# Two mixers of a decode kernel: the Gelu tiles summed on VectorE, and the small work placed at half chunks

## The chip, the cores and the metric

The kernel runs on one core of one Trainium2 chip. The engines that matter here are TensorE (PE in the profile, with PEld for its weight loads), VectorE (DVE), ScalarE (ACT), GpSimd (POOL), and the 16 DMA engines, which bring data from the chip's memory into SBUF. All large loads are issued in program order on the queue of SyncE (SPq in the profile, q1 in its list of DMA queues). PSUM holds the banks that TensorE accumulates into. The metric is the device time of one execution in microseconds.

## The reference

Two layers, each an attention with a long K and V cache and a mixer, for one new token of two batch items:

```python
def _A_ref(x, k_cache, v_cache, wq, wo):
    q = (x @ wq).reshape(B, 1, 32, 128)                 # 32 heads, transposed to (B, heads, 1, 128)
    k = jnp.repeat(k_cache, 4, axis=1)                  # 8 K/V heads, 32768 keys of 128
    v = jnp.repeat(v_cache, 4, axis=1)
    p = _softmax(einsum("bhqd,bhkd->bhqk", q, k) * (128 ** -0.5))
    return einsum("bhqk,bhkd->bhqd", p, v).reshape(B, 1, 4096) @ wo
def _B_ref(x, w1, b1, w2, b2):                          # token mixing, one token, F = 1792
    h = _layernorm(x)                                   # (B, 1, 512)
    u = _gelu(einsum("bsd,sf->bdf", h, w1) + b1)        # (B, 512, 1792)
    return transpose(einsum("bdf,fs->bds", u, w2) + b2) # (B, 1, 512)
x = A_x
for layer in range(2):
    x = x + _A_ref(_layernorm(x), A_k_cache, A_v_cache, A_wq, A_wo)
    x = x + _B_ref(_layernorm(x), B_w1, B_b1, B_w2, B_b2)
```

Both layers use the same caches and weights, so each batch item and head is read twice, apart from what the kernel keeps on chip in between.

## The kernel before

**Units and chunks.** A unit is one layer, one batch item and one K/V head: 32 of them, in an order fixed by `units`. Each unit has 8 chunks of 4096 keys for K and 8 for V. A chunk is 2 MB. `k_chunk` (L416) multiplies the unit's four queries with a chunk, 16 products into one PSUM tile of scores for each of two groups of four chunks; after each group VectorE takes the maxima (L426). When all K of a unit is through, `max_1` and `max_2` find the maxima over all keys (L432, L436, L438, L442, L444), the scores are turned (L448) into the SBUF tiles S0 and S1, ScalarE exponentiates them (L453, or all at once L465 and L468), and `v_chunk` (L558) multiplies them with the V chunks, 16 products of 128x512 each into the PSUM bank `acc`. At the unit's end `out_1` sums four masked blocks of `acc` on VectorE (L526, L528, `add_blocks`), multiplies with a selector (L595) and divides (L597); `out_2` multiplies with the head's part of wo and accumulates four rows in the PSUM bank `rows` (`add_row`, L238). The query of a unit comes from `make_q`: products with wq (L340), a copy (L349), four transposing products (L352) and a copy.

**Memory.** SBUF has 13 cells of 2 MB in `mem` (and a rest). Most chunks are loaded two or four at a time (4 and 8 MB). Between the units N1 and N3 fewer cells are free, since weights and a part of the cache that both layers use stay on chip: there the loads are of one chunk, or of two half chunks where no whole cell has been free for long enough (`spread`, `half`). A load into a cell waits for the products that last read it, so the order of TensorE's work decides when the next loads can start.

**The changes of layer and batch.** N1 is the last unit of layer 0 of batch item 0, N2 that of layer 0 of batch item 1. After each the mixer has to run, and the next but one unit (N1 + 2, N2 + 2) needs its result for its query. The unit in between (N1 + 1, N2 + 1) can already be computed. In the stream of chunks its K comes behind the last V of N1 or N2, its V behind that, and the resident K chunk of the unit after (kept on chip from layer 0, so without a load) among them. Because `rows` carries both batch items, the mixer works on rows: `take_rows` copies `rows` to S1 (L609) and clears them (L610), `mix_1` puts the layer's input into the PSUM bank `bcast` on all partitions, `mix_2` adds the attention's result with a selector product (L641), takes the statistics of the layer norm (L644 to L649, the power on GpSimd, L630) and makes scale and bias columns. A Gelu tile (`hidden_tile`, L780) is one ScalarE operation on `bcast`, 128 hidden units by 512 channels, and there are 14 of them. `hidden_out` multiplies each with its column of w2 and accumulates in `rows` (L238 again). `mix_4` adds the result to `bcast` by a selector product (L792), copies it (L799) and takes the statistics (L801 to L804); `to_columns` (L304) turns it into the columns from which `make_q` works.

**The order of work.** There is no automatic scheduler: each engine runs its instructions in the order in which the program issues them. The last loop goes through the stream of chunks. For each it issues the load, then the chunk's products, advances the time `t` by one and issues whatever `at(time, f, ...)` has put there, by rank. The load of a chunk is issued when its turn in this stream comes; how far it runs ahead of the products is settled by when its cell is read out. In the mixers of N1 and N2 the numbers in `BURSTS` say how many of the 14 `hidden_out` products, each followed by a later Gelu, stand behind each K chunk. `ASIDE` shifts the V chunks of N1 + 1 and N2 + 1 to three places earlier in the stream, and `SOONER` brings two V loads of N2 ahead of two K loads.

Of the kernel before, what the change touches and what calls it, by code (L numbers as in the profile page):

```python
# [9 lines left out]
AF = mybir.ActivationFunctionType  # L10
# [18 lines left out]
ASIDE = 3  # L29
BURSTS = (0, 3, 3, 3, 4, 1)  # L30
# [14 lines left out]
def gqa_mixer_kernel(ctx: ExitStack, tc: tile.TileContext, x, kt, v, wqo, cols, out):  # L45
# [279 lines left out]
    def make_q(n, step, place=None):  # L325
# [40 lines left out]

    SOONER = {(N2, 6): (N2, 1), (N2 + 1, 0): (N2, 3)}
# [38 lines left out]
    def k_chunk(n, c):  # L406

        kc = k_at.pop((n, c))
        half, i = divmod(c, PACK)
        if i == 0:  # L410
            sc_ps[n, half] = pscore.tile([P, 512], F32, name="scores")
        for k in range(SUB):
# [10 lines left out]
        if i == PACK - 1:  # L423
# [123 lines left out]
    def v_chunk(n, c):  # L547
        very_last = n == NU - 1 and c == NCH - 1
        vc = v_at.pop((n, c))
# [5 lines left out]
        for q in range(quads):  # L555
# [8 lines left out]
            )  # L564
        if very_last:
            add_tiles()
# [220 lines left out]

    def mix_4(key):
# [8 lines left out]
        else:  # L797
            ysb[key] = row_tile()
            nc.vector.tensor_copy(ysb[key], p)  # L799
            st, mv, rs = ln_st[:, :6], ln_mv, ln_rs  # L800
            nc.vector.bn_stats(st, p)  # L801
            nc.vector.bn_aggr(mv, st)
            nc.vector.tensor_scalar_add(rs, mv[:, 1:2], EPS)
            nc.gpsimd.tensor_tensor(rs, rs, half_neg, op=ALU.pow)  # L804
            stats[key] = mv, rs
# [45 lines left out]
    for n in range(NU):  # L851
# [4 lines left out]
        if n:  # L856
            if n in (N1 + 2, N2 + 2):
                q0 = q1 = mixed[layer - 1, b]
                place = S[1]
            else:  # L860
                place = S[0] if n in (N2 + 1, N3 + 1) else None
                q0 = kbeg[n] - (10 if n == N3 + 1 else 6)
                q1 = q0 + 1
            q2 = q1 + 1
            assert q2 <= kbeg[n]
            at(q0, make_q, n, 0)
            at(q1, make_q, n, 1)
            at(q2, make_q, n, 2, place)
            if place is S[0]:
# [3 lines left out]
        if n in (N1 + 1, N2 + 1):  # L873
            at(kend, max_1, n, 0)
            at(kend, max_2, n)
            at(kend, exponentials_at_once, n, 0)
            t1 = mixed[units[n - 1][:2]] + 1
# [4 lines left out]
        else:  # L882
# [4 lines left out]
            if n == N2:  # L887
# [17 lines left out]
        at(vend if change else min(vend + 1, vbeg[n + 1]), out_1, n)  # L905
        at(vend if change or n == NU - 2 else vend + 2, out_2, n)
# [125 lines left out]
```

## Time and profile before

| | |
|---|---|
| runs | 2498.47, 2500.21, 2500.77 us; median 2500.21 |
| profiled execution | 2501.7 us, span 2499.9 us |
| TensorE, mean granted clock | 0.766 |
| TensorE busy | 1400.0 us, 56% of the span |
| VectorE busy | 222.9 us, 9% |
| ScalarE busy | 185.6 us, 7% |
| read from the chip's memory | 1063.81 MB |

Shares of time are of the profiled execution's span. In the page's section of 40 slices a slice is 62.5 us; the two mixers that the diff touches lie at about 1145 to 1195 us and 1337 to 1385 us. The rows of the profile that the argument uses are shown with the prediction. A row of the timeline has the start and the duration in us, the engine, the line, the operation, the tiles as output<-inputs, the shapes, the count, and in brackets the engine's idle time before it with what ended it. A row of a table by stretch has the stretch, its length, for PE, PEld, DVE, ACT and POOL the busy time with the number of instructions, the mean granted clock of TensorE, the busy share of the DMA engines, and the GB/s that they moved. A row of a group has its line, engine, operation, tiles and shapes, the count, the busy time with the mean of one in ns, and the engine's idle time before it with its releasers.

### The profile page before, as it was taken

How to read it: one execution, taken by the hardware profiler on the slowest of the kernel's cores; microseconds unless marked ns; L12 is line 12 of the kernel's file. 1: busy time of each engine (PE TensorE's matmuls, PEld its weight loads, DVE VectorE, ACT ScalarE, POOL GpSimd, SP SyncE). 2: the span in 40 equal slices, each digit the busy share in tenths (PEclk: the TensorE clock that was granted, in tenths of full speed). 3: DMA queues.
4: the chain of work that ended last, by engine and by line, in shares of the span. 5: the costliest groups of instructions: out<-in, count | busy, mean ns of one | idle time of the engine just before them, and what ended most of it. 6: DMA issues, size and time to landing. Idle time of an engine off the chain costs nothing.

```text
span 2499.9 us, 20566 instructions
## 1 busy us (share of the span) xinstructions
PE 1400.0 (56%) x9326; PEld 380.2 (15%) x9326; DVE 222.9 (9%) x610; ACT 185.6 (7%) x550; POOL 4.9 (0%) x17
## 2 busy tenths in 40 slices
PE   4545554645445554667667775465545554456547
PEld 1111111111111111111111111111111111111112
DVE  0000000000000000001111110000000000010102
ACT  0000000000000000001012010000000000011002
POOL 0000000000000000000000000000000000000000
PEclk8777777777777777879888887677778777777778
DMA  9999999999999999999999999999999999999996
GB/s 419 436 433 427 435 436 429 436 430 430 433 434 434 433 429 434 424 425 416 426 424 415 427 428 432 430 433 432 433 434 433 430 430 433 434 431 433 430 432 271
DMA packets 34656, 1065.14 MB, mean 426 GB/s; under 512 B 4101, under 2 KB 4105, under 8 KB 5002
## 3 DMA queue, kind: packets, MB, share of 16 engines
q1 hardware_dynamic: 34280, 1063.80, 99.1%
q8 instruction: 73, 1.20, 0.2%
q14 instruction: 13, 0.11, 0.0%
q10 hardware_dynamic: 290, 0.04, 0.0%
HBM read 1063.81 MB, written 0.00 MB: 426 GB/s over the span
## 4 chain that ended last, share of the span: by engine, by line
DMA 72%; PE 26%; DVE 1%; ACT 1%; issue 0%; SPq 0%; POOL 0%; ACTq 0%
DMA mem<-in_v_dram 37%; DMA mem<-in_kt_dram 35%; PE scores L416 11%; PE acc L558 11%; PE rows L238 1%; PE kept L340 1%; PE bcast L340 0%; ACT S L780 0%; PE small L595 0%; PE small L442 0%; PE small L587 0%; PE kept L737 0%; PE small L352 0%; PE bcast L641 0%; DVE S L528 0%
## 5 line engine op out<-in xcount | busy, mean ns | idle before, releaser
L416 PE MATMUL scores<-mem,small_sb 128*32 128x512 f32 x4096 | 636.8, 735 | 597.4 <-DMA mem<-in_kt_dram 596.9
L558 PE MATMUL acc<-mem,S 128*16 128x512 f32 x4088 | 615.5, 739 | 445.1 <-DMA mem<-in_v_dram 439.4
L416 PEld LDWEIGHTS scores<-mem,small_sb 128*32 128x32 f32 x4096 | 153.4, 129 | 983.9 <-issue 907.9
L453 ACT ACTIVATE S<-S,small_sb 128x128 f32<-128x128 f32 x240 | 123.6, 519 | 2096.9 <-DVE small_sb L444 1627.0
L558 PEld LDWEIGHTS acc<-mem,S 128*16 128x16 f32 x4088 | 134.8, 111 | 808.0 <-issue 678.8
L426 DVE TENSOR_REDUCE small_sb<-scores 128x1 f32<-128x512 f32 x64 | 44.2, 691 | 870.2 <-PE scores L416 870.2
L448 DVE STREAM_TRANSPOSE S<-scores 128x512 f32<-128x512 f32 x64 | 45.4, 710 | 129.4 <-PE acc L558 129.4
L238 PE MATMUL rows<-mem,small_sb 128*1 128x512 f32 (+1 forms) x276 | 50.5, 637 | 3.1 <-ACT mem L780 2.4
L340 PE MATMUL kept<-mem,small_sb 128*2 128x512 f32 x104 | 51.2, 618 | 1.7 <-DVE small_sb L266 1.7
L453 ACT ACTIVATION_READ_ACCUMULATOR S<-S,small_sb 128x1 f32 x240 | 44.8, 187 | 0.0
L438 DVE TENSOR_REDUCE small_sb<-small 1x4 f32<-1x128 f32 x32 | 8.8, 276 | 271.7 <-PE small L436 271.7
L528 DVE SCALAR_TENSOR_TENSOR S<-acc,small_sb,S 128x128 f32<-128x128 f32 x93 | 32.6, 351 | 3.3
L589 DVE RECIPROCAL small_sb<-small 128x4 f32<-128x4 f32 x32 | 5.9, 185 | 286.5 <-PE small L587 286.5
L597 DVE TENSOR_TENSOR small_sb<-small,small_sb 128x4 f32<-128x4 f32 x31 | 5.1, 164 | 292.9 <-PE small L595 292.9
L780 ACT ACTIVATE S<-bcast,small_sb 128x512 f32<-128x512 f32 x28 | 20.7, 775 | 95.6 <-DVE small_sb L649 83.1
L238 PE MATMUL rows<-S,small_sb 128*1 128x512 f32 (+1 forms) x56 | 21.3, 592 | 8.0 <-ACT S L780 8.0
L352 PE MATMUL small<-small_sb,mem 2*128 2x2 f32 x112 | 15.1, 252 | 17.9 <-DVE mem L349 17.9
L526 DVE TENSOR_SCALAR S<-acc,small_sb 128x128 f32<-128x128 f32 x31 | 10.8, 350 | 138.0 <-PE acc L558 138.0
L595 PEld LDWEIGHTS small<-small_sb,S 128*128 128x128 f32 x62 | 12.6, 255 | 51.6 <-issue 40.5
L340 PE MATMUL bcast<-mem,small_sb 128*1 128x512 f32 (+1 forms) x40 | 18.5, 592 | 1.2 <-DVE small_sb L309 1.2
L352 PEld LDWEIGHTS small<-small_sb,mem 2*128 2x128 f32 x112 | 13.9, 190 | 30.5 <-DVE mem L349 27.3
L595 PE MATMUL small<-small_sb,S 128*128 128x4 f32 x62 | 15.4, 318 | 4.9 <-DVE S L528 4.9
(132 smaller groups left out, 272.4 us busy)
## 6 DMA issues: line engine op xcount, KB each, us to landing
mem<-in_kt_dram SPq DMA_DIRECT2D x33, 2048.0 KB, 17.6
mem<-in_v_dram SPq DMA_DIRECT2D x20, 2048.0 KB, 20.7
mem<-in_v_dram SPq DMA_DIRECT2D x9, 4096.0 KB, 29.8
mem<-in_v_dram SPq DMA_DIRECT2D x29, 1024.0 KB, 10.5
mem<-in_wqo_dram SPq DMA_DIRECT2D x14, 2048.0 KB, 33.7
mem<-in_kt_dram SPq DMA_DIRECT2D x7, 4096.0 KB, 27.2
mem<-in_kt_dram SPq DMA_DIRECT2D x22, 1024.0 KB, 8.7
mem<-in_v_dram SPq DMA_DIRECT2D x2, 1280.0 KB, 29.2
```

Source lines behind the costliest of these rows:

```text
L238: nc.tensor.matmul(rows[32 * g : 32 * g + b + 1, :], weights if b else weights[:, 1:], row, start=False, stop=True, skip_group_check=True,)
L340: nc.tensor.matmul(q_ps[n][:m, :], xnT[:, d, b : b + m], wq_at(h)[:, d, :], start=(d == 0), stop=(d == DT - 1),)
L352: nc.tensor.matmul(pt[:, r * m : (r + 1) * m], q_row[n][:m, r * DH : (r + 1) * DH], ident[:m, :m], start=True, stop=True,)
L416: nc.tensor.matmul(sc_ps[n, half][32 * g : 32 * g + 32, :], q, kc[k * NG + g], start=(i == 0 and k == 0), stop=(i == PACK - 1 and k == SUB ...
L426: nc.vector.tensor_reduce(mx[n][:, half : half + 1], sc_ps[n, half], axis=AX.X, op=ALU.max)
L448: nc.vector.transpose(S[half], sc_ps[n, half])
L453: nc.scalar.activation(s[:, :, h], s[:, :, h], AF.Exp, bias=neg[n][:, h : h + 1], scale=SCALE, accum_out=lsum[n][:, half, h : h + 1],)
L526: nc.vector.tensor_scalar_mul(t, acc[:, :DH], mask[:, 0:1])
L528: nc.vector.scalar_tensor_tensor(t, acc[:, k * DH : (k + 1) * DH], mask[:, k : k + 1], t, op0=ALU.mult, op1=ALU.add)
L558: nc.tensor.matmul(acc[32 * g : 32 * g + R * QT, :], S[half][:, col : col + R * QT], vc[q], start=(c == 0 and q < NG), stop=(c == NCH - 1 ...
L595: nc.tensor.matmul(po[:, :R], asb, selh, start=True, stop=True)
L780: nc.scalar.activation(hid[key, f], px[key], AF.Gelu_apprx_tanh, bias=shift[key][:, f : f + 1], scale=slope[key][:, f : f + 1],)
```

## The change

Six things, all in the stretch of the two mixers, except that half chunks are now a general unit of the order:

- `k_chunk` and `v_chunk` issue a half chunk at a time (`part`), and `run(t + 0.5)` issues small work between the halves of a chunk that stands alone. `make_q` has four steps instead of three: the copy and the transposing products are apart. `out_1` is split in `out_0` (the block sums on VectorE) and `out_1` (the product and the division). At N1 and N2 `out_0` stands behind the last V, `out_1` half a chunk later, `out_2` one chunk later; `mix_1` keeps its place a chunk ahead of V's end, and the copy of `rows` and `mix_2` stand 1 and 1.5 chunks behind it.
- In place of the bursts there is `hidden_sum`: each Gelu tile, in S0 or S1 by turns, is multiplied by its column of w2 and added to `acc` on VectorE (the last into its own tile). `acc` is free there, since N1 + 1 (N2 + 1) has not started its V. The load of the Exp table follows the Gelus on ScalarE.
- `mix_3` sums over the partitions with one product with ones, straight into `bcast`, so that `mix_4`'s copy of `rows` and its selector product are not needed there; its copy to S1 is on ScalarE. `statistics` is what stood in `mix_4`.
- The mixer's result is placed at `vend + 4.5` and `vend + 5`, ahead of the last K halves of N1 + 1 (N2 + 1), the query of the unit after behind it, at `vend + 5.5` and `vend + 6`.
- The V chunks of N1 + 1 and N2 + 1 come behind the resident K chunk of the unit after, not three places earlier: that chunk now follows the unit's K, and `max_1`, `max_2` and the exponentials stand at the end of K and half a chunk later. The first scores are turned when the mixer's result is there.
- `SOONER` is gone, and the plan of which cell a load takes follows from the new order.

```diff
-ASIDE = 3
-BURSTS = (0, 3, 3, 3, 4, 1)
...
-            if step == 2:
+            if step == 3:
...
         if step == 2:
             q_row[n] = spot() if place is None else place
             nc.vector.tensor_copy(q_row[n][:m, :], q_ps[n][:m, :])
+        if step == 3:
             pt = misc()
...
-    SOONER = {(N2, 6): (N2, 1), (N2 + 1, 0): (N2, 3)}
...
-    def k_chunk(n, c):
+    def k_chunk(n, c, part):
...
-        for k in range(SUB):
+        for k in (part,):
...
-    def max_1(n, turned=None):
+    def max_1(n):
         mxa = field(n, HALVES, 1)
         nc.vector.tensor_reduce(mxa, mx[n], axis=AX.X, op=ALU.max)
-        if turned is not None:
-            turn_scores(n, turned)
...
-    def v_chunk(n, c):
+    def v_chunk(n, c, part):
...
-        for q in range(quads):
+        for q in range(part * NG, min(quads, (part + 1) * NG)):
...
+        if part < SUB - 1:
+            return
...
+    def out_0(n):
+        add_blocks(row_tile()[:, :DH])
     def out_1(n):
-        asb = row_tile()[:, :DH]
-        add_blocks(asb)
         po = misc()
-        nc.tensor.matmul(po[:, :R], asb, selh, start=True, stop=True)
+        nc.tensor.matmul(po[:, :R], row_tile()[:, :DH], selh, start=True, stop=True)
...
+    def hidden_sum(key):
+        for f in range(FT):
+            h, w = S[f % HALVES], w2z[:, f, 1:]
+            hidden_tile(key, f, h)
+            if f == 0:
+                nc.vector.tensor_scalar_mul(acc, h, w)
+            else:
+                nc.vector.scalar_tensor_tensor(
+                    h if f == FT - 1 else acc, h, w, acc, op0=ALU.mult, op1=ALU.add
+                )
+        nc.scalar.activation(unread, one, AF.Exp)
+    def mix_3(key):
+        p = px[key]
+        nc.tensor.matmul(p, ones, S[(FT - 1) % HALVES], start=False, stop=True, skip_group_check=True)
+        ysb[key] = row_tile()
+        nc.scalar.activation(ysb[key], p, AF.Copy)
+        statistics(key)
+    def statistics(key):
+        st, mv, rs = ln_st[:, :6], ln_mv, ln_rs
+        nc.vector.bn_stats(st, px[key])
+        nc.vector.bn_aggr(mv, st)
+        nc.vector.tensor_scalar_add(rs, mv[:, 1:2], EPS)
+        nc.gpsimd.tensor_tensor(rs, rs, half_neg, op=ALU.pow)
+        stats[key] = mv, rs
...
-                key = (n + 1) * NCH - 0.5 + max(c / (2 * NCH) - 0.5, c - ASIDE + 1)
+                key = (n + 1) * NCH - 0.5 + max(c / (2 * NCH) - 0.5, c + 1)
...
-                q0 = q1 = mixed[layer - 1, b]
+                q0 = q1 = q2 = mixed[layer - 1, b] + 0.5
+                q3 = q2 + 0.5
...
-            at(kend, max_1, n, 0)
-            at(kend, max_2, n)
-            at(kend, exponentials_at_once, n, 0)
-            t1 = mixed[units[n - 1][:2]] + 1
+            t0 = mixed[units[n - 1][:2]]
+            at(t0, turn_scores, n, 0, rank=2)
+            at(kend, max_1, n)
+            at(kend + 0.5, max_2, n)
+            at(kend + 0.5, exponentials_at_once, n, 0)
+            t1 = kend + 1
+            assert t0 + 1 <= kend == kbeg[n + 1]
             at(t1, turn_scores, n, 1, rank=2)
...
-            if n == N2:
+            if n in (N2, N3):
                 t0 = max(t0, kbeg[n + 1] - 3)
...
-        at(vend if change else min(vend + 1, vbeg[n + 1]), out_1, n)
-        at(vend if change or n == NU - 2 else vend + 2, out_2, n)
+        at(vend if change else min(vend + 1, vbeg[n + 1]), out_0, n)
+        at(vend + 0.5 if change else min(vend + 1, vbeg[n + 1]), out_1, n)
+        at(vend + 1 if change else vend if n == NU - 2 else vend + 2, out_2, n)
         if units[n] == lay[layer, b][-1]:
             key = (layer, b)
-            begin = vend + (1 if change else 3)
-            at(begin - 2 if change else vend, mix_1, key)
-            at(begin - 1, take_rows, key, row_tile())
-            at(begin, mix_2, key)
-            at(vend + 1, gelu_table)
+            at(vend - 1 if change else vend, mix_1, key)
+            at(vend + (1 if change else 2), take_rows, key, row_tile())
+            at(vend + (1.5 if change else 3), mix_2, key)
+            at(vend + (0 if change else 1), gelu_table)
             if change:
-                assert k_done[n + 1, NCH - 1] == begin + len(BURSTS) - 1 and sum(BURSTS) == FT
-                places = S
-                through = [begin + k for k, m in enumerate(BURSTS) for _ in range(m)]
-                for f in range(len(places)):
-                    at(begin, hidden_tile, key, f, places[f], rank=2)
-                for f, w in enumerate(through):
-                    at(w, hidden_out, key, f, rank=0)
-                    if f + len(places) < FT:
-                        at(w, hidden_tile, key, f + len(places), places[f % len(places)], rank=0)
-                e = begin + len(BURSTS) - 1
+                assert k_done[n + 1, NCH - 1] == vend + 6
+                at(vend + 2, hidden_sum, key, rank=2)
+                at(vend + 4.5, mix_3, key)
+                at(vend + 5, to_columns, key)
+                mixed[key] = vend + 5
...
-        if not is_v and (n, c) in SOONER:
-            load_v(*SOONER[n, c], m, limit)
-        if not is_v or (n, c) not in SOONER.values():
-            (load_v if is_v else load_k)(n, c, m, limit)
+        (load_v if is_v else load_k)(n, c, m, limit)
         for j in range(m):
-            (v_chunk if is_v else k_chunk)(n, c + j)
+            for part in range(SUB):
+                (v_chunk if is_v else k_chunk)(n, c + j, part)
+                if m == 1 and part == 0:
+                    run(t + 0.5)
```

More of the change, by code (lines that the diff above doesn't have):

```diff
@@ L404, in load_k @@
             k_at[n, c + j] = at[j * (JT // QT) : (j + 1) * (JT // QT)]
[L406 to L408 removed]
+    def k_chunk(n, c, part):
+        kc = k_at[n, c]
         half, i = divmod(c, PACK)
[L410 removed]
+        if i == 0 and part == 0:
             sc_ps[n, half] = pscore.tile([P, 512], F32, name="scores")
[L412 removed]
+        for k in (part,):
             at = R * (SUB * i + k)
@@ L422, in k_chunk @@
                 )
-        if i == PACK - 1:
+        if i == PACK - 1 and part == SUB - 1:
             if half == 0:
@@ L799, in mix_4 @@
             nc.vector.tensor_copy(ysb[key], p)
[L800 to L805, printed above, removed]
+            statistics(key)
     def parts(n, with_v):
@@ L949, in gqa_mixer_kernel @@
         for c in KEPT:
-            first = next((k_done[k] - 1 for k, e in SOONER.items() if e == (n, c)), v_done[n, c] - 1)
-            book(KEPT[c][1], 2 if KEPT[c][0] > QT else 1, first)
+            book(KEPT[c][1], 2 if KEPT[c][0] > QT else 1, v_done[n, c] - 1)
     closed[WCELL0], closed[WCELL0 - 1] = kbeg[N2 + 1], kbeg[N3 + 2] - 8
@@ L954, in gqa_mixer_kernel @@
     first_input()
-    for step in range(3):
+    for step in range(4):
         make_q(0, step)
```

19 lines of the change are left out of this document (10 added, 9 removed).

## The prediction

> **What bounds the kernel now.** I read the page's busy lines first, then the transfer rates by stretch, then the chain of waits, and then the order of time around the two mixers.
>
> ```profile
> span 2499.9 us, 20566 instructions
> ...
> PEclk8777777777777777879888887677778777777778
> DMA  9999999999999999999999999999999999999996
> GB/s 419 436 433 427 435 436 429 436 430 430 433 434 434 433 429 434 424 425 416 426 424 415 427 428 432 430 433 432 433 434 433 430 430 433 434 431 433 430 432 271
> ...
> q1 hardware_dynamic: 34280, 1063.80, 99.1%
> ...
> DMA 72%; PE 26%; DVE 1%; ACT 1%; issue 0%; SPq 0%; POOL 0%; ACTq 0%
> ...
> mem<-in_v_dram SPq DMA_DIRECT2D x29, 1024.0 KB, 10.5
> ...
> mem<-in_kt_dram SPq DMA_DIRECT2D x22, 1024.0 KB, 8.7
> ```
>
> The transfers fill every slice but the last. The changed kernel moves the same bytes, so time can only come from stretches where the transfer engines pause or move bytes less well, and can only be lost by new pauses. The weak slices are 17 to 22, the stage with the two mixers that the diff touches. Stretches of it (engine columns, then PE clock, transfer share, GB/s):
>
> ```profile
> 600.00:900.00 300.00, 158.21 (x1086) 42.78 (x1078) 22.14 (x64) 17.20 (x64) 0.00 (x0) 0.75 1.00 432
> 1150.00:1155.00 5.00, 4.83 (x34) 1.04 (x26) 2.18 (x7) 0.00 (x0) 0.54 (x1) 0.91 0.81 315
> 1160.00:1195.00 35.00, 28.90 (x178) 8.00 (x176) 8.86 (x19) 9.27 (x13) 0.54 (x1) 0.95 1.01 421
> 1210.00:1260.00 50.00, 30.83 (x190) 6.70 (x182) 5.01 (x14) 4.14 (x16) 0.00 (x0) 0.81 1.01 428
> 1151.00:1151.50 0.50, 0.50 (x12) 0.11 (x4) 0.00 (x0) 0.00 (x0) 0.00 (x0) 1.00 0.55 229
> 1343.50:1344.00 0.50, 0.50 (x8) 0.00 (x0) 0.00 (x0) 0.00 (x0) 0.00 (x0) 0.50 0.70 295
> ```
>
> Three things cost rate here. While all loads are 1 MB halves (1160 to 1195) the full queue moves 421 GB/s; with 2 MB chunks (1210 to 1260) 428. In the first mixer five microseconds ran at a share of 0.81, a pause of 0.95 us; in the second the share dips to 0.70 for about a microsecond, some 0.3 us. The whole inventory is therefore about 1.3 us of pauses and fractions of a microsecond in packing: a gain of 5 us is not there to be had.
>
> **Why the first pause exists.** In order of time:
>
> ```profile
> 1143.46 1.91 PE L558 MATMUL acc<-mem,S 128*16 128x512 f32 x16 [1.90 <-DMA mem<-in_v_dram]
> 1145.44 0.35 DVE L526 TENSOR_SCALAR S<-acc,small_sb 128x128 f32<-128x128 f32 x1 [15.38 <-PE acc L558]
> 1147.64 1.89 PE L238 MATMUL rows<-mem,small_sb 128*1 128x512 f32 x8 [0.25 <-DVE small_sb L597]
> 1148.45 0.20 PEld L416 LDWEIGHTS scores<-mem,small_sb 128*32 128x32 f32 x4 [0.70 <-DMA mem<-in_kt_dram]
> 1149.30 2.71 PE L416 MATMUL scores<-mem,small_sb 128*32 128x512 f32 x16
> 1151.23 13.01 SPq L138 DMA_DIRECT2D mem<-in_kt_dram  x7
> 1153.11 0.70 DVE L644 BATCH_NORM_STATS2 small_sb<-bcast 128x6 f32<-128x512 f32 x1 [2.16 <-PE bcast L641]
> 1153.24 0.16 PEld L416 LDWEIGHTS scores<-mem,small_sb 128*32 128x32 f32 x8 [1.00 <-DMA mem<-in_kt_dram]
> 1155.49 1.45 ACT L780 ACTIVATE S<-bcast,small_sb 128x512 f32<-128x512 f32 x2 [47.55 <-DVE small_sb L649]
> ```
>
> After the last V chunk the PE waits for the block sums and the row products, then takes a K chunk that had landed at 1148.45; the load into that cell is issued at 1151.23, when part of the engines have run dry. Data flow again near 1152.5, so issue to data takes about 1.25 us.
>
> **The change, part by part.**
>
> *Small work at half chunks.* The first K half goes ahead of the block sum's product and the row products: from 1148.45, half of 2.71 us, to 1149.8. The next load is issued 1.4 us sooner. The share never falls below 0.55, so engines with the most left never paused, and a load ends only with its last engine: the gain lies between nothing and the whole 0.95 + 0.3 us. I take 0.3, near the lower end.
>
> *Load sizes.* The page's last rows above count 29 + 22 loads of 1 MB; the changed program's order has 17 + 18. Sixteen halves become eight chunks: 16.78 MB at 428 instead of 421 GB/s, 39.20 for 39.85 us, a gain of 0.65 us. The rest of the queue (weights, V pieces of 1.25, 0.75 and 0.25 MB) keeps its sizes.
>
> *Gelu tiles summed on VectorE.* Gone from the PE are the hidden products: 28 records of 592 ns for each mixer, which stood between K halves that mostly waited for transfers. In their place come 14 VectorE operations, one after the other through acc:
>
> ```profile
> L238 PE MATMUL rows<-S,small_sb 128*1 128x512 f32 x28 | 10.6, 592 | 3.9 <-ACT S L780 3.9
> L780 ACT ACTIVATE S<-bcast,small_sb 128x512 f32<-128x512 f32 x14 | 10.3, 775 | 54.5 <-DVE small_sb L649 47.6 <-PE rows L238 6.9
> L610 DVE TENSOR_SCALAR rows<-rows,small_sb 128x512 f32<-128x512 f32 x2 | 1.5, 750 | 0.0
> L465 DVE SCALAR_TENSOR_TENSOR S<-S,small_sb 128x512 f32<-128x512 f32 x2 | 1.4, 693 | 0.1
> ```
>
> A multiply-add with acc in and out is not in this trace; the nearest are 693 ns (same operation, tiles in SBUF) and 750 ns (PSUM to PSUM). I take 750. With two S tiles a Gelu waits for the sum two tiles back, so two tiles take 775 + 750 ns and four hand-overs of some 40 ns, 0.84 us a tile; ScalarE alone would need 0.82. I take 0.82: 14 tiles last 13 x 0.82 + 0.78 + 0.75 = 12.2 us. The first Gelu also comes later: the row products end near 1153.0, their copy at 1153.7, the product with the selector stands behind half of the K chunk that lands at 1153.24 and ends at 1155.3, and 2.38 us of statistics (1153.11 to 1155.49) bring it to 1157.7. The sum ends at 1169.9.
>
> *What waits behind the sum.* The PE waits there with the mixer's last product (the new L803), and behind it in its queue stand the K halves, the columns, q, the maxima, the resident K chunk and the first V half, the last two of which release the next loads. Now the V half starts 5 us after the last K half lands:
>
> ```profile
> 1173.14 0.30 PEld L416 LDWEIGHTS scores<-mem,small_sb 128*32 128x32 f32 x8 [0.56 <-DMA mem<-in_kt_dram]
> 1178.18 3.60 PE L558 MATMUL acc<-mem,S 128*16 128x512 f32 x16 [1.65 <-ACT S L468]
> 1182.76 1.91 PE L558 MATMUL acc<-mem,S 128*16 128x512 f32 x16
> 1182.87 0.69 DVE L799 COPY S<-bcast 128x512 f32<-128x512 f32 x1 [4.14 <-PE bcast L792]
> 1184.61 1.05 PE L304 MATMUL small<-small_sb,S 128*128 128x1 f32 x8
> 1184.65 0.54 POOL L804 TENSOR_TENSOR small_sb<-small_sb 128x1 f32<-128x1 f32 x1 [29.82 <-DVE small_sb L803]
> 1186.25 3.16 PE L340 MATMUL bcast<-mem,small_sb 128*1 128x512 f32 x7 [0.60 <-DVE small_sb L309]
> 1191.49 1.05 PE L352 MATMUL small<-small_sb,S 1*128 1x1 f32 x8
> ...
> 1335.10 3.50 PE L558 MATMUL acc<-mem,S 128*16 128x512 f32 x16 [1.90 <-DMA mem<-in_v_dram]
> ...
> 1365.01 0.31 PEld L416 LDWEIGHTS scores<-mem,small_sb 128*32 128x32 f32 x8 [0.54 <-DMA mem<-in_kt_dram]
> ```
>
> From the end of the sum: its product 1.1, the copy to SBUF on ScalarE 0.8, statistics and the power on GpSimd 2.05, q's products 3.6 (the seven records and the eighth), a K half 0.96 (half of 1.91), the turn of q 1.05, the maxima (small operations as at L432, L436, L442, some 0.2 to 0.4 each) 0.8, half the resident chunk 0.96, one more small product 0.4: 11.6 us. Then 0.96 for the other half of the resident chunk; or, beside that, 1.6 for the exponentials and 0.96 for the first V half.
>
> *When that is too late.* A ring of five 1 MB cells feeds this stretch, 2.49 us each at 421 GB/s. In the first mixer five halves follow the last K half: 1173.14 + 12.45 = 1185.6 is when the queue is dry, less 1.25 from issue to data and 0.3 for the issue: 1184.0 is the latest release. It needs the first V half: 1169.9 + 11.6 + 2.56 = 1184.05. In the second four halves follow, then a load into the resident chunk's cell: 1365.01 + 9.96 - 1.55 = 1373.4. There the selector's product again stands behind the second K chunk, which lands two 2 MB transfers (4.9 us each at 428) after the last V chunk's 1335.1, at 1344.9: first Gelu 1349.4, end of the sum 1361.6, release 1374.2. So 0.05 and 0.8 us late if the PE keeps its full clock. Now the hidden products keep it busy; in the changed order it waits some 3 us before L803, and the V rows at 1178.18 and 1182.76 show the same work at 3.60 after such a wait and 1.91 soon after. I add that difference, 1.69, to each: 1.75 + 2.5 = 4.25 us of pauses, where all engines wait, late ones too.
>
> *The resident K chunk and V later.* The V halves of this unit now follow its K by half a chunk and more, and the chunks behind alternate over five 2 MB cells: four transfers of 4.9 us stand behind each release, and PE work per chunk is under 4 us, so I cost this at nothing; without that depth it would be the same pause again. The early turn of the first score tile (0.7 us) hides behind transfers.
>
> *Sum:* 4.25 - 0.65 - 0.3 = +3.3 us. The profiled execution took 2501.7 us around its span of 2499.9, so 2505.0; it lies 1.5 above the runs' median of 2500.21, on which the forecast stands: 2503.5.
>
> **Rivals.**
> 1. *The chain fits.* The PE stays warm, or the sum runs at 0.78 us a tile (0.5 us less): pauses 0.3 to 0.85 us, less 0.95 to 1.9 of gains, 2498.8 to 2500.3, say 2499.5. For it: the releases are late by under 1 us in my own walk. Against it: 3.60 us at 1178.18.
> 2. *The PE at half clock through the chain* (the slower side). If the waits for copy and statistics keep it from warming, the product (1.07), the K half (0.96), the columns (0.97) and half of q (1.7) double: 4.7 us more instead of 1.69, so 4.75 + 5.5 - 0.95 = +9.3, 2509.5. It decides from about 3.2 us of extra chain in both mixers. For it: the late slices have clocks of 0.7 to 0.8. Against it: q's products now run warm at 1186 straight after such waits.
> [...]
> 3. *More than the pauses is won*, over 5 us: nothing in the rows offers it unless the stage's whole deficit goes (421 to 432 over the halves, plus pauses).
>
> **How the numbers follow.** Forecast 44% (its own range 2501 to 2506), chain fits 24%, half clock 25%, large gain 7%. A measurement of this kernel tells about 0.2% (5.0 us) from no change: slower beyond 2505.2 takes the half clock and a tenth of the forecast, 29%; faster 7%; the rest, 64%, within. The range 2498.0 to 2509.5 leaves out half of the half-clock case and the gain.
>
> **What would show it.** Right: in the first mixer L803 starts near 1170 after an idle PE, the share dips between 1184 and 1188, and near 1374 in the second; the dips at 1150 and 1343 shrink; 17 + 18 loads of 1 MB; acc's multiply-adds near 750 ns, one each 0.82 us. Wrong: no dip at either place (rival 1), q's products at twice their time (rival 2), or multiply-adds over 0.9 us, which would lengthen both pauses by over 1 us.

## The result and the profile after

| | before | changed |
|---|---|---|
| runs beside each other, us | 2498.47 to 2500.77, median 2498.74 (5) | 2506.59 to 2512.43, median 2510.26 (5) |
| profiled execution, us | 2501.7 (span 2499.9) | 2510.26 (span 2508.5) |

The changed kernel is slower: a ratio of 1.004, 95% interval 1.0025 to 1.0055. Its median lies 0.8 us above the upper end of the predicted range, and its runs are spread over 6 us, those of before over 2.

The page of the changed kernel, its lines that answer to those of before:

```profile
span 2508.5 us, 20487 instructions
...
PEclk8777777777777777888797887777777777777778
...
GB/s 419 433 433 433 434 434 431 432 429 434 432 433 432 433 429 432 430 426 381 426 426 404 395 428 433 433 433 432 430 432 431 432 429 430 434 432 435 433 431 285
...
q1 hardware_dynamic: 33128, 1063.80, 98.8%
...
mem<-in_kt_dram SPq DMA_DIRECT2D x18, 1024.0 KB, 9.2
mem<-in_v_dram SPq DMA_DIRECT2D x17, 1024.0 KB, 10.4
```

The loads are those counted in advance, 18 + 17 of 1 MB. The loss is in three slices: 19 (381 GB/s, 416 before), 22 and 23 (404 and 395, before 415 and 427). Transfer rates by stretch in the changed kernel (stretch, length, the engines' busy times, TensorE's granted clock, DMA share, GB/s):

```profile
1150.00:1160.00 10.00, 6.58 (x50) 1.26 (x42) 4.86 (x11) 2.10 (x3) 0.54 (x1) 1.00 0.98 380
1160.00:1180.00 20.00, 13.98 (x65) 3.31 (x66) 11.38 (x20) 10.76 (x15) 0.54 (x1) 0.74 0.98 395
1182.00:1192.00 10.00, 9.34 (x82) 2.84 (x86) 4.98 (x9) 1.26 (x2) 0.00 (x0) 1.00 0.80 265
1344.00:1354.00 10.00, 8.80 (x52) 2.06 (x52) 3.36 (x10) 0.16 (x1) 0.54 (x1) 0.83 1.00 417
1354.00:1364.00 10.00, 6.00 (x32) 0.71 (x32) 8.62 (x12) 9.05 (x12) 0.00 (x0) 0.74 1.02 424
1376.00:1386.00 10.00, 9.03 (x62) 2.99 (x64) 5.56 (x11) 1.26 (x2) 0.00 (x0) 1.00 0.40 144
```

And the same of the kernel before, where the second mixer lies 4.4 us sooner:

```profile
1150.00:1160.00 10.00, 8.47 (x55) 2.24 (x49) 3.12 (x9) 3.62 (x5) 0.54 (x1) 0.95 0.91 369
1340.00:1350.00 10.00, 8.14 (x46) 2.11 (x46) 3.84 (x11) 1.27 (x2) 0.54 (x1) 0.83 0.97 379
1350.00:1360.00 10.00, 8.18 (x57) 2.49 (x56) 0.00 (x0) 6.13 (x10) 0.00 (x0) 1.00 1.01 408
```

Against the 421 GB/s that a full queue of half chunks moved before, the changed kernel lost 20 x 26 / 421 = 1.2 us in 1160 to 1180, 3.7 us in 1182 to 1192 and 6.6 us in 1376 to 1386: 11.5 us. At the old pauses it won back 10 x 11 / 421 = 0.3 us in the first mixer and (38 + 16) x 10 / 421 = 1.3 us in the second. With 0.65 us for packing, an amount that I only worked out, that makes +9.3; the spans differ by 8.6. The near match owes something to the choice of stretches: from 1160 to 1200 (366 GB/s, before 420) and from 1365 to 1395 (312, before 424) the loss is 5.1 + 8.0 = 13.1 us, the same sum then gives +10.9, and the medians differ by 11.5. So the sum is good to about 2 us. (In a pause the share is too mild a reading: 0.80 in 1182 to 1192 stands beside 265 of 421 GB/s.) The two places are those that the prediction named (1184 to 1188, and near 1374, which the first pause moves to 1378).

The clock has changed too: 0.74 in 1160 to 1180, where it was 0.95 in 1160 to 1195. The second mixer's chain in order of time, from the sum's adds to the resident K chunk whose end releases the next load:

```profile
1355.51 10.21 DVE L795 SCALAR_TENSOR_TENSOR acc<-S,small_sb,acc 128x512 f32<-128x512 f32 x12
...
1366.62 2.08 PE L803 MATMUL bcast<-S,small_sb 128*128 128x512 f32 x2 [2.96 <-DVE S L795]
...
1368.62 1.94 PE L413 MATMUL scores<-mem,small_sb 128*32 128x512 f32 x8
...
1370.49 1.87 PE L302 MATMUL small<-small_sb,S 128*128 128x1 f32 x8
...
1372.29 1.93 PE L413 MATMUL scores<-mem,small_sb 128*32 128x512 f32 x8
...
1374.00 4.08 PE L338 MATMUL bcast<-mem,small_sb 128*1 128x512 f32 x7
...
1382.13 1.06 PE L413 MATMUL scores<-mem,small_sb 128*32 128x512 f32 x8
```

The sum behaves nearly as worked out: 12 multiply-adds in 10.21 us, 0.85 each, and L803 waits for it. But L803, two K halves and the columns (L302) each take about twice what the prediction's rows had: 2.08, 1.94, 1.87 and 1.93 us, and q's products (L338) take 4.08 us, where the row of before had 3.16. The granted clock was 0.50 from 1366.6 to 1374.0 and 0.78 from there to 1378.1. In the first mixer L803 starts near 1170 after an idle TensorE, as the prediction asked:

```profile
1170.53 2.08 PE L803 MATMUL bcast<-S,small_sb 128*128 128x512 f32 x2 [3.82 <-DVE S L795]
...
1185.20 1.91 PE L553 MATMUL acc<-mem,S 128*16 128x512 f32 x16 [0.65 <-ACT S L463]
```

Of this chain only L803 and the K half behind it (1.94 us) are slow there: the columns take 1.05 us and q's products 3.17 again; the clock was 0.50 from 1170 to 1174 and 1.00 from 1174.5 to 1180.

### The profile page after: what moved, and what is told of

The parts are those of the page before. It is cut to its first block, busy times and chain, and to the rows that moved or that the text cites. A ratio compares the mean times of both kernels' runs of the same rounds, so it can differ in the third digit from the quotient of the medians.

```text
span 2508.5 us, 20487 instructions
## 1 busy us (share of the span) xinstructions
PE 1386.6 (55%) x9270; PEld 372.2 (15%) x9270; DVE 239.9 (10%) x632; ACT 188.0 (7%) x554; POOL 4.9 (0%) x17
## 4 chain that ended last, share of the span: by engine, by line
DMA 73%; PE 24%; DVE 1%; issue 1%; ACT 0%; SPq 0%; POOL 0%; DVEq 0%; ACTq 0%
DMA mem<-in_v_dram 37%; DMA mem<-in_kt_dram 36%; PE scores L413 11%; PE acc L553 10%; PE kept L338 1%; DVE acc L795 1%; PE rows L236 0%; PE bcast L338 0%; PE small L437 0%; PE small L593 0%; PE bcast L803 0%; PE small L584 0%; PE kept L735 0%; PE small L351 0%; PE small L302 0%
## 5 line engine op out<-in xcount | busy, mean ns | idle before, releaser
L338 PE MATMUL kept<-mem,small_sb 128*2 128x512 f32 x104 | 51.0, 616 | 1.7 <-DVE small_sb L264 1.7
L338 PE MATMUL bcast<-mem,small_sb 128*1 128x512 f32 (+1 forms) x40 | 19.4, 617 | 0.0
L795 DVE SCALAR_TENSOR_TENSOR acc<-S,small_sb,acc 128x512 f32<-128x512 f32 x24 | 18.1, 755 | 2.5
L431 PE MATMUL small<-small_sb 128*1 128x128 f32 x64 | 16.1, 343 | 0.6 <-DVE small_sb L429 0.6
```

Source lines behind the costliest of these rows:

```text
L338: nc.tensor.matmul(q_ps[n][:m, :], xnT[:, d, b : b + m], wq_at(h)[:, d, :], start=(d == 0), stop=(d == DT - 1),)
L431: nc.tensor.matmul(pm[:1, :P], mxa, ident, start=True, stop=True)
L795: nc.vector.scalar_tensor_tensor(h if f == FT - 1 else acc, h, w, acc, op0=ALU.mult, op1=ALU.add)
```

## The experiments

The ratio beside each run is against the kernel before on the same chip. Unless the text says otherwise, the kernel is the changed one with the edit shown.

### A second execution of the changed kernel

No edit.

> The changed kernel once more, for a second look. Theory (two late releases, their size set by how cold TensorE runs through the mixer's chain): the share of the DMA engines dips at the same two places, near 1185 and near 1380 us, and nowhere new; the time differs from the 2510.26 us of the first look by about what the two dips differ. Rival (a loss spread over the stage, by load sizes or their order): the dips agree with the first look and the time moves without them.

Measured: 2511.55 us. Its rates by stretch:

```profile
1160.00:1180.00 20.00, 14.35 (x54) 3.73 (x55) 11.34 (x19) 10.82 (x15) 0.54 (x1) 0.57 0.98 397
1182.00:1192.00 10.00, 9.04 (x76) 3.21 (x75) 6.55 (x13) 1.26 (x2) 0.00 (x0) 1.00 0.57 201
1376.00:1386.00 10.00, 9.03 (x52) 2.84 (x54) 3.95 (x9) 0.63 (x1) 0.00 (x0) 0.93 0.45 155
```

The dips are at the same two places: by the sum above, 1.1 + 5.2 + 6.3 = 12.6 us where the first execution had 11.5, and the time is 1.3 us longer. The first pause is larger by 1.5 us than it was there, with a clock of 0.57 ahead of it instead of 0.74: the columns, the K half behind them and q's products are slow here (1.87, 1.93 and 3.91 us), and the first V chunk starts 2.4 us later.

```profile
1187.64 1.91 PE L553 MATMUL acc<-mem,S 128*16 128x512 f32 x16 [0.65 <-ACT S L463]
```

So between these two executions the time moves with the pauses, and the first pause with the clock.

### TensorE kept busy while it waits

```diff
+                for w, k in ((2.5, 4), (3, 4), (3.5, 4), (4, 4), (4.5, 10)):
+                    at(vend + w, idle_products, k, rank=0)
                 at(vend + 4.5, mix_3, key)
```

> Products of the identity with itself stand between the K halves and ahead of the mixer's last product, while TensorE waits for the sum: 4 behind each of four halves and 10 ahead of the last product. Theory (a cold TensorE makes the second release later): the last product, the K halves and the columns behind it take about 1.1 us instead of 1.9 to 2.1 in the second mixer, the second pause shrinks from 6.0 to about 2.5 us, the first by up to 1 us, and the time comes to about 2505 us. Rival (the clock is beside the path, the order of waits alone is to blame): no change, 2508 to 2512 us.

Measured: 2501.8 us, ratio 1.0009 (1.0000 to 1.0018). The second mixer's chain in order of time:

```profile
1363.54 1.12 PE L803 MATMUL bcast<-S,small_sb 128*128 128x512 f32 x2 [1.41 <-DVE S L795]
...
1364.59 1.07 PE L413 MATMUL scores<-mem,small_sb 128*32 128x512 f32 x8
...
1365.59 1.05 PE L302 MATMUL small<-small_sb,S 128*128 128x1 f32 x8
...
1367.52 3.16 PE L338 MATMUL bcast<-mem,small_sb 128*1 128x512 f32 x7
...
1374.74 1.07 PE L413 MATMUL scores<-mem,small_sb 128*32 128x512 f32 x8
```

Its rates at both places, and within the second pause:

```profile
1179.00:1189.00 10.00, 9.04 (x79) 3.42 (x82) 5.91 (x12) 1.26 (x2) 0.00 (x0) 1.00 0.90 331
1372.00:1382.00 10.00, 9.04 (x78) 3.31 (x82) 5.86 (x12) 1.26 (x2) 0.00 (x0) 1.00 0.76 297
1374.00:1375.00 1.00, 1.00 (x11) 0.45 (x10) 0.15 (x1) 0.00 (x0) 0.00 (x0) 1.00 0.45 188
1375.00:1376.00 1.00, 0.81 (x8) 0.00 (x0) 0.97 (x3) 0.23 (x1) 0.00 (x0) 1.00 0.02 8
```

The products of the identity with itself (`idle_products`, which the last mixer of the kernel has long used) compute nothing that is read; they only occupy TensorE. With the clock at 1.00 (1352 to 1382) the same chain, L803 to the end of the resident K chunk's second half, lasts 1363.54 to 1375.81, 12.3 us; in the changed kernel it lasted 1366.62 to 1383.19, 16.6 us. In the first mixer, from L803 (1170.70) to the end of the first half of V (which starts at 1183.63), it lasts 13.9 us; in the changed kernel 15.6. The ratio falls by 0.0031, 7.8 us, more than the 5 that I expected of it. What stays, 2.2 us against before, is about what dips of 2.1 us in the first place (331 of 421) and 2.9 in the second (297) leave when the old pauses and the packing have given back theirs. The last two rows show how the queue dries up: a share of 0.45 and then 0.02, so about half of the DMA engines' time is already empty in the microsecond before the queue stands still.

### Fewer tiles in the sum

```diff
+        n_f = FT // 2 + 1
-        for f in range(FT):
+        for f in range(n_f):
...
-                    h if f == FT - 1 else acc, h, w, acc, op0=ALU.mult, op1=ALU.add
+                    h if f == n_f - 1 else acc, h, w, acc, op0=ALU.mult, op1=ALU.add
```

> Only 8 of the 14 Gelu tiles are computed and summed in the two mixers; 6 tiles of hidden units are left out. Theory (the releases wait for a chain that begins with the sum): the sum ends 5.1 us sooner (6 tiles of 0.85), the first dip goes and the second shrinks to under 1 us, the time is 2500 to 2502 us. Rival (the loss lies in load sizes, the order of loads or VectorE's writing to PSUM): the dips stay, over 2506 us.

The run leaves out 6 of the 14 tiles, so its output is not the reference's. Measured: 2499.19 us, ratio 0.9998 (0.9989 to 1.0007). The rates at the two places, which lie sooner here:

```profile
1180.00:1190.00 10.00, 9.35 (x90) 2.53 (x82) 4.27 (x7) 1.26 (x2) 0.00 (x0) 1.00 0.99 400
1368.00:1378.00 10.00, 9.04 (x76) 3.23 (x72) 6.51 (x13) 1.26 (x2) 0.00 (x0) 1.00 0.83 324
```

The first pause is all but gone (400 GB/s), of the second 2.3 us are left (324), a microsecond more than expected. Loads, their order and VectorE's way of adding in PSUM are the changed kernel's here, and the time is that of before. So the loss is the chain's lateness, and none of these three. TensorE was not warm for it: in the second mixer the last product (L804 in this file) still took 2.08 us, for 1.12 in the run with TensorE kept busy.

### The VectorE sum alone, in the kernel before

```diff
             if change:
...
+                at(begin, hidden_sum, key, rank=2)
                 e = begin + len(BURSTS) - 1
...
+            if change:
+                at(e, mix_3, key)
+            else:
+                at(e, take_rows, key, None, rank=2)
+                at(e + 1, mix_4, key)
```

> The kernel before with one part of the change alone: the Gelu tiles summed on VectorE and the mixer's last product by ones; the old order of chunks, loads and small work stays, with three V chunks ahead of the resident K chunk. Theory (the sum costs nothing by itself, what hurts is that V and the resident chunk wait behind the chain that it begins): the dips are those of before (near 1151 and 1343 us) and none follows, 2497.5 to 2500.5 us. Rival (the sum on VectorE is itself the cost): 2503 us or more.

Measured: 2504.32 us, ratio 1.0016 (1.0006 to 1.0025). By its number that is the rival's. In order of time around the first mixer's last K half:

```profile
1173.27 1.93 PE L416 MATMUL scores<-mem,small_sb 128*32 128x512 f32 x8 [1.42 <-DMA mem<-in_kt_dram]
...
1175.13 1.91 PE L805 MATMUL bcast<-S,small_sb 128*128 128x512 f32 x2
...
1181.74 6.20 PE L558 MATMUL acc<-mem,S 128*16 128x512 f32 x32 [1.65 <-ACT S L468]
```

The last product (L805 in this file) had come between the last K half and the maxima (L436), in 1.91 us where the run with TensorE kept busy had 1.12, and its statistics with it: the first V half starts at 1181.74, before it was 1178.18. I had put it a place ahead of where its counterpart, L792, stood. So this run could not tell the sum from its place, and the next one was made for that:

```diff
-                at(e, mix_3, key)
+                at(e - 1, mix_3, key)
```

> The kernel before with the Gelu tiles summed on VectorE, as in the earlier run of that part alone, but the mixer's last product stands one K chunk earlier, where the sum has just ended, and no longer between the last K half and the first V half. Theory (the 4.8 us of the earlier run came from that place: product and statistics stood ahead of the maxima and made the first V half 3.5 us later): no dip near 1185 or 1375, 2498 to 2500.5 us. Rival (the sum itself costs, by a cold TensorE or VectorE's time): 2503 us or more, as in the earlier run.

Measured: 2499.25 us, ratio 1.0001 (0.9992 to 1.0010). In order of time, K halves (L416) and the first V chunks (L558) of the first mixer:

```profile
1163.15 1.07 PE L416 MATMUL scores<-mem,small_sb 128*32 128x512 f32 x8 [1.42 <-DMA mem<-in_kt_dram]
...
1165.63 1.93 PE L416 MATMUL scores<-mem,small_sb 128*32 128x512 f32 x8 [1.42 <-DMA mem<-in_kt_dram]
...
1177.97 4.48 PE L558 MATMUL acc<-mem,S 128*16 128x512 f32 x24 [1.64 <-ACT S L468]
```

And its rates over the same time:

```profile
1160.00:1180.00 20.00, 12.89 (x70) 2.32 (x70) 11.44 (x20) 9.43 (x13) 0.54 (x1) 0.81 1.01 422
```

V starts at 1177.97, where it started at 1178.18 before, and up to 1190 no dip follows. TensorE is cold here too (a clock of 0.81, and the K half at 1165.63 takes 1.93 us), and the time is that of before. In this order q's products take 4.86 us in the first mixer, with a clock of 0.70 from 1180 to 1190. A small loss does stand further on, in the second mixer, where it was 420 GB/s before:

```profile
1380.00:1390.00 10.00, 9.73 (x72) 3.14 (x74) 4.62 (x8) 0.63 (x1) 0.00 (x0) 0.97 0.97 381
```

That is some 0.9 us; in return this mixer moves 423 GB/s from 1350 to 1360, where it was 408 before. So the VectorE sum is not a cost in the time (1.0001), and the clock of 0.81 cost little in this order, where the releases hardly wait for what runs at it.

### V ahead of the resident K chunk

```diff
-                key = (n + 1) * NCH - 0.5 + max(c / (2 * NCH) - 0.5, c + 1)
+                key = (n + 1) * NCH - 0.5 + max(c / (2 * NCH) - 0.5, c)
...
-            at(kend + 0.5, max_2, n)
-            at(kend + 0.5, exponentials_at_once, n, 0)
+            at(kend, max_2, n)
+            at(kend, exponentials_at_once, n, 0)
```

> The changed kernel with one part undone: the unit's first V chunk comes ahead of the resident K chunk again (the exponentials stand at the end of K, as before); the mixer's last product, its columns and the query stay ahead of the last K halves. Theory (releases wait for a chain of sum, last product, columns and query on a cold TensorE): in the first mixer the first V half still waits for the query's products, only half a chunk sooner, so its pause stays within 1 us of the changed kernel's; in the second the five half cells carry one load more before the queue is dry, so the pause of 6 us becomes 3 to 4; 2505 to 2508 us. Rival (the resident chunk ahead of V is the whole loss): both pauses go, 2498 to 2500 us.

Measured: 2513.54 us, ratio 1.0057 (1.0043 to 1.0070). Neither theory had that. In order of time, the last K half and the first V chunk of the first mixer:

```profile
1182.15 1.42 PE L413 MATMUL scores<-mem,small_sb 128*32 128x512 f32 x5
...
1187.64 3.32 PE L553 MATMUL acc<-mem,S 128*16 128x512 f32 x16 [1.65 <-ACT S L463]
```

I had reckoned that V would start half a chunk sooner. It starts at 1187.64, just where it did in the second execution of the changed kernel (1185.20 in the first): in both orders V waits for the exponentials (L463). With the resident chunk behind V, TensorE has nothing to do in that wait, and the V half behind it takes 3.32 us, for 1.91 in the changed kernel's second execution. So the part that moved the resident K chunk ahead of V shows no loss where the query stands ahead of the last K half; it covers a wait. Whether it is a gain is not clear, since the intervals of this run and of the changed kernel (1.0025 to 1.0055) overlap. The last K half itself (1182.15) is late behind the query, which no order of V mends.

### The last product, the columns and the query later

In addition to the edit that puts V ahead:

```diff
-                at(vend + 4.5, mix_3, key)
-                at(vend + 5, to_columns, key)
-                mixed[key] = vend + 5
+                at(vend + 5, mix_3, key)
+                at(vend + 5.5, to_columns, key)
+                mixed[key] = vend + 5.5
```

> As the run with V ahead of the resident chunk, and the mixer's last product, columns and query half a chunk later, so that the last K halves and the maxima stand ahead of the columns and the query. Theory: the first V half waits for the last K half, the maxima and the query's products alone, some 8 us behind the landing of the last K half where 10.9 are allowed; both pauses near 1185 and 1380 go even with a cold TensorE, the dip near 1151 stays; 2498 to 2501 us. Rival (a cold TensorE makes it late in any order): a pause of over 1.5 us in at least one mixer, 2502 us or more.

Measured: 2504.75 us, ratio 1.0022 (1.0013 to 1.0031): the rival. Then the same with four products of the identity behind each of six K halves:

> The same with products of the identity (4 behind each of six K halves) that keep TensorE's clock up. Theory: where no release is late the clock is off the path, so this run is within 1 us of the one without these products, 2498 to 2500 us. Rival (the clock decides by itself): at least 2 us faster than the run without them.

Measured: 2503.99 us, ratio 1.0013 (1.0005 to 1.0022). The median is 0.8 us below that of the run without these products, and not near the 2498 to 2500 that I expected. The executions fall in two groups, four from 2498.2 to 2500.7 and seven from 2503.1 to 2504.4. A second profiled execution, no edit:

> The run with V ahead, the later product and warm K halves once more, for a second look, since its times fell near 2498.5 in some executions and near 2504 in others. Theory (the later times come from query products that run cold, as in the run without the products of the identity): where the time is near 2504, the query's products take over 4 us instead of 3.2 in one mixer and a pause follows there. Rival (something else in the stage): 3.2 us in both mixers and a pause all the same.

Measured: 2503.84 us. The query's products (L338) in the first mixer, without the products of the identity:

```profile
1178.76 6.13 PE L338 MATMUL bcast<-mem,small_sb 128*1 128x512 f32 x7
```

The same with them, in an execution of 2498.8 us:

```profile
1176.85 3.17 PE L338 MATMUL bcast<-mem,small_sb 128*1 128x512 f32 x7
```

And in the second profiled execution of that kernel, both mixers:

```profile
1178.03 4.86 PE L338 MATMUL bcast<-mem,small_sb 128*1 128x512 f32 x7
...
1370.53 6.12 PE L338 MATMUL bcast<-mem,small_sb 128*1 128x512 f32 x7
```

Seven products take 3.17 us where the clock is 1.00 (from 1170 to 1190 in the execution of 2498.8 us), and 6.13 and 6.12 us where it is 0.76 (1180 to 1190 without the products of the identity) and 0.67 (1370 to 1380 in the second execution); V stands behind them. The K halves between the products of the identity took 1.06 and 1.07 us in the second execution, and in the first mixer the clock was 1.00 from 1160 to 1170, 0.93 in the ten us behind and 0.90 in the next ten. So the drop comes at the end of the wait for the maxima, 1.6 us of idle with 0.4 of work between, or in the query itself. The execution of 2498.8 us has the same wait and no drop (1.00). So four more products of the identity went there:

```diff
-                for w, k in ((2.5, 4), (3, 4), (3.5, 4), (4, 4), (4.5, 4), (5, 4)):
+                for w, k in ((2.5, 4), (3, 4), (3.5, 4), (4, 4), (4.5, 4), (5, 4), (6, 4)):
```

> As the run with V ahead, the later product and warm K halves, and 4 more products of the identity where TensorE waits for the maxima, ahead of the query. Theory: the query's products then run at full clock in nearly all executions, the times near 2504 us become rare and the median is 2498 to 2499.5 us. Rival (the two groups of times have nothing to do with that wait): both groups stay, median 2501 to 2504 us.

Measured: 2500.43 us (2498.09 to 2502.01), ratio 1.0003 (0.9995 to 1.0012). The group near 2504 is gone; the median is 0.9 us above what I expected, and with before inside the interval this is no gain.

### Busy only ahead of the last product

The changed kernel with the 10 products at `vend + 4.5` alone.

> The changed kernel with the 10 products of the identity ahead of the mixer's last product alone, and none between the K halves. Theory: a busy stretch of 3 to 5 us right ahead of the chain brings the clock back for the chain itself, so most of the 8.5 us of the run with products at all places comes back: 2502 to 2505 us. Rival (the clock is set by the K halves' gaps over a longer time): the last product and the K half behind it still take 1.9 us or more, over 2507 us.

Measured: 2503.69 us, ratio 1.0019 (1.0010 to 1.0027). The first mixer in order of time, the products of the identity (L683) and L803:

```profile
1167.70 4.24 PE L683 MATMUL small<-small_sb 128*128 128x128 f32 x20
...
1171.78 1.02 PE L803 MATMUL bcast<-S,small_sb 128*128 128x512 f32 x2
```

The ten products (20 records) take 4.24 us, where they took 2.50 with TensorE busy all along. The K half ahead of them takes 1.94 us, L803 and the K half behind them 1.02 and 1.07. The clock was 0.56 from 1160 to 1170 and 0.93 from 1170 to 1180. In this mixer they end 1.1 us after the sum, which is done at 1170.7, so they make the chain later as well. Two thirds of what the full set brought are there.

### The query behind the first V half

V ahead as above, with `mix_3` at `vend + 5`, the columns at `vend + 6`, the query from there, and no products of the identity.

> No products of the identity: V ahead of the resident chunk, the mixer's last product half a chunk later, and the query's products behind the first V half, so that the release of the next load no longer waits for them. Theory (order alone can take the clock off the path): the first V half ends some 6.5 us after the last K half lands although TensorE runs cold, and the pause of 3.9 us that the run with the query ahead of V had in the first mixer goes; the load behind it waits for the second V half, behind the query, 2.5 us later, so up to 1.5 us may come back where the query runs cold; 2498.5 to 2501.5 us. Rival (a cold TensorE costs as much in this order): over 2503 us, as with the query ahead.

Measured: 2506.65 us, ratio 1.0031 (1.0021 to 1.0042): a miss. The first mixer in order of time:

```profile
1179.64 1.05 PE L553 MATMUL acc<-mem,S 128*16 128x512 f32 x8 [1.64 <-ACT S L463]
...
1180.51 4.86 PE L338 MATMUL bcast<-mem,small_sb 128*1 128x512 f32 x7
...
1185.22 1.43 PE L553 MATMUL acc<-mem,S 128*16 128x512 f32 x5
```

The rate in the second mixer:

```profile
1380.00:1390.00 10.00, 9.71 (x87) 3.29 (x81) 4.64 (x8) 0.63 (x1) 0.00 (x0) 1.00 0.59 224
```

The first V half ended at 1180.7, well in time. But the next load waits for the second V half, now behind q's cold products (4.86 us), at 1186.6. In the second mixer, where the same order stands, 4.7 us are lost (224 GB/s). I had seen that wait and allowed 1.5 us for it. The kernel before has three V chunks ahead of the resident K chunk; one half ahead of the query is too few.

No version tried here beats the kernel before by more than its runs differ.

## Why the prediction went as it did

- *Where.* This was right: DMA-bound, the two pauses at the places named, both from releases behind the mixer's chain; no gain to be had beyond a microsecond or two.
- *The sum.* First Gelu 1157.7 predicted, 1157.75 in the trace; the end 1169.9 predicted, 1170.5. I took 0.82 us a tile, ScalarE's bound; the other count, 0.84 with the hand-overs, is what came (0.85). The price of an add in PSUM, 750 ns, held (755).
- *The chain at full clock.* 11.6 + 0.96 = 12.6 us were predicted for the second mixer, and the run with TensorE kept busy had 12.3. (The terms that I listed add up to 11.7, not 11.6; the slip is too small to matter.)
- *The clock's share of it.* This is the step that failed: "I add that difference, 1.69, to each". The cold chain cost 16.6 - 12.3 = 4.3 us in the second mixer, in both profiled executions; in the first, from L803 to the end of the first V half, 1.7 us in the first execution (15.6 against 13.9) and 4.1 in the second. I assumed that one piece of work runs cold and the clock is back after it. That held by size for the first mixer of the first execution; in the other three cases four to five pieces run cold. The second rival had them one by one, 4.7 us, and I had given it 25%. That its 2509.5 us lies so near to the measured time is in part luck: it counts 4.7 us in both mixers, where the first execution had 1.7 and 4.3, and the next item makes up the rest. Its sign, q's products at twice their time, did not come either (3.17 and 4.08 us for 3.16). Against it I had held that q's products ran at full clock at 1186 before. TensorE had worked on V ahead of them there; but in the run with the sum alone and its product early it did so too, and q took 4.86 us, so what kept q fast before stays open.
- *When the queue is dry.* Mis-sized by some 2 us for each mixer: at full clock I counted 0.05 and 0.8 us of lateness, the run with TensorE kept busy still has dips of 2.1 and 2.9. I took the landing of the last load for the end of the queue, but the engines' mean share has fallen to half (0.45) about a microsecond sooner. The sum's end, 0.6 us later than counted in the first mixer, is in it too; how the 2 us divide was not measured.
- *The gains.* The old pauses gave back 0.3 + 1.3 us where I took 0.3 in all and allowed 1.25. The packing's 0.65 was not measured by itself.
- *The resident K chunk ahead of V.* I costed it at nothing. Undoing it gave no faster kernel (1.0057 for 1.0040, with intervals that overlap), so it is no loss in this order.

The prediction asked what covers the work that is taken away, and named transfers. The hidden products on TensorE had a second use, which I wrote down ("Now the hidden products keep it busy") and then priced for one piece of work: they kept its clock up for the chain behind them (0.96 from 1160 to 1180 before, 0.74 and 0.57 in the two executions of the changed kernel). Shown by runs: with TensorE busy again, 7.8 of the 10 us go; with the chain 5 us shorter, all of it goes, although part of the chain still runs cold.

## What to carry to other kernels

Before taking work off TensorE where it is idle half of the time, look whether that work keeps its clock up for a serial chain that follows, and price the whole chain at half clock until a row shows where the clock is back: here the chain took 16.6 us for 12.3, with K halves of 1.93 us for 1.07. The low clock cost time here where a release waited behind it: moving the chain off the path of the next load (the VectorE sum in the old order, 1.0001) was worth as much as keeping the engine warm (1.0009), and there the times did not fall apart into groups. In a ring of buffers that is just deep enough, an order has to be checked for every release in turn, not for the first (the query behind the first V half lost 4.7 us at the second release).

## What the runs showed of the hardware

TensorE's clock fell without any long wait. In the kernel with the sum alone and its product early, K halves of 1.06 us came every 2.41 to 2.49 us, with idle gaps of 1.3 to 1.4 us, and after four of them that took 1.06 or 1.07 us the fifth took 1.93 (the fourth and the fifth are the rows at 1163.15 and 1165.63 above): no gap was longer than 1.5 us, and TensorE was busy for 43% of the time. With 2.2 us of work in every 2.49 us, in the run with TensorE kept busy, the clock was 1.00 from 1160 to 1170; in the kernel before, busy for 14.75 of the 20 us from 1160 to 1180, it was 0.96. How much work it takes to hold the clock was not measured.

Executions of one kernel differ in it. In two executions of the changed kernel the clock from 1160 to 1180 was 0.74 and 0.57, and the first mixer's pause 3.7 and 5.2 us; the kernel with V ahead, the later product and warm K halves had 1.00 from 1170 to 1190 in an execution of 2498.8 us, and 0.93 from 1170 to 1180 and 0.90 from 1180 to 1190 in one of 2503.84. What makes this difference no run shows.
